# Transposes moved to another PSUM bank, and the last product of a feed-forward block in two column halves

## The chip, the cores and the metric

The kernel runs on one core of a Trainium2 chip. A core has five engines that run their own instruction queues and meet through semaphores: TensorE (PE in the profile, its weight loads PEld), VectorE (DVE), ScalarE (ACT), GpSimd (POOL) and SyncE (SP, which here only issues DMAs). Matmul results go to PSUM, eight banks of 512 fp32 values per partition; VectorE and ScalarE copy them out. The metric is device time of the whole program in microseconds (us), lower is better, and a kernel's time is the median of several runs.

## The reference

Clustered attention, followed by a feed-forward block with a leaky activation. Queries and keys are assigned to the nearest of 16 centroids per head; a query attends only to keys of its own cluster.

```python
q_assign = np.argmax(np.einsum('bhsd,hcd->bhsc', q_n, c_n), axis=-1)
k_assign = np.argmax(np.einsum('bhsd,hcd->bhsc', k_n, c_n), axis=-1)
mask = q_assign[:, :, :, None] == k_assign[:, :, None, :]
scores = scale * np.matmul(q, k.transpose(0, 1, 3, 2))
scores = np.where(mask, scores, -1000000000.0)
attn = np.exp(scores - np.max(scores, axis=-1, keepdims=True))
attn = attn / (np.sum(attn, axis=-1, keepdims=True) + 1e-09)
attn_out = np.matmul(attn, v)
x = attn_out.transpose(0, 2, 1, 3).reshape(B * S, H * D)
h = x @ w_in
g = np.maximum(h, 0.0) + alpha * np.minimum(h, 0.0)
out = g @ w_out
```

There are 4 batches (B), 8 heads (H), 768 tokens (S), head dimension 64; the model width DM is 512 and the hidden width 2048.

## The kernel before

Heads go in pairs, four pairs per batch, 16 in all (n = 0 to 15). For the first three batches each pair is computed whole: scores by matmul, exp on ScalarE, a mask on VectorE, the product with v on TensorE, and a division by row sums. For the last batch (n = 12 to 15) the tokens of each head are first sorted by cluster, so that each block of 128 keys needs only its neighbouring blocks of queries. The sorted result must then go back to token order. This way back is:

- `normalise_near` (L929) multiplies the two halves of the pair's result by the inverse sums and puts the rest into the plan with `later(slots, piece)`: `to_rows` for the first half 6 slots on, for the second half 9 slots on.
- `to_rows` (L951) transposes three 128x128 blocks of a half on TensorE (L955) into one PSUM bank; one slot later ScalarE copies them to `rows` (L958).
- `put_back` (L961) scatters rows to DRAM by an indirect DMA on GpSimd's queue (L963), 12 per pair; `fetch_back` (L968) loads them again by four DMAs on SP's queue (L975), and VectorE turns them into `xT` (L985).

Around this runs the feed-forward block of the batch before. `ffn_pieces` (L1000) makes a list of pieces per half batch: `hidden(f)` (L1013) makes 128 hidden units by four matmuls (L1017), which ScalarE copies out of PSUM as `gT` (L1023) and VectorE gives its slope (L1009); `final(i, f0, ...)` (L1028) multiplies the gT of several f with w_out (L1035). After the first eight f its result is copied to `y` (L1041), after the second eight it is added (L1043) and stored by SP (L1046). The main loop takes a slot at a time: it runs what is due (`tick`), then a piece of the attention, then as many feed-forward pieces as the plan wants (`feed`). Every engine runs its instructions in the order in which this program wrote them.

PSUM's eight banks are shared out by hand: `ps_s` two tiles of two banks for scores (`sps`), `ps_v` one bank (`vps`) for the product with v, `ps_m` one bank (`mps`) and `ps_f` two banks (`fps`). `fps` holds the feed-forward pieces, two of six score blocks in the last batch, and the transposes of `to_rows`. `mps` is what `misc()` (L84) gives: the sums over rows (`total`, L848), the cluster numbers (`prep_clusters`, L442), the second side of the product with v in the sorted batch (L926), and the small products of the check at the end (L1283, L1319). A new tile in a bank waits until the last reader of the tile before it has finished.

At the very end a flag `bad` is read by every engine (L1326), and all jump over a general version of the kernel that these inputs do not need (L1451). The last feed-forward half batch (b = 3, half = 1) runs alone there, after all attention: 8 hidden pieces, 6 final pieces, twice.

Of the kernel before, what the change touches and what calls it, by code (L numbers as in the profile page):

```python
# [10 lines left out]
FP32 = mybir.dt.float32  # L11
# [5 lines left out]
ALU = mybir.AluOpType  # L17
AX = mybir.AxisListType
PS = bass.MemoryType.PSUM
P = 128  # L20
# [3 lines left out]
def kernel(  # L24
# [11 lines left out]
    nc = tc.nc  # L36

    B, H, S, D = q.shape
    NC = centroids.shape[1]
    DM, DF = moe_w_in.shape  # L40
    NJ = S // P
    NCH = DM // P
    NF = DF // P
    HJ = NJ // 2
# [12 lines left out]
    w_out_sb = wpool.tile([P, NF, DM], FP32, name="w_out_sb")  # L57
# [9 lines left out]
    accp = fast.enter_context(tc.tile_pool(name="accp", bufs=2))  # L67
# [7 lines left out]
    ps_f = fast.enter_context(tc.tile_pool(name="ps_f", bufs=2, space=PS))  # L75
# [8 lines left out]
    def misc():  # L84
        if early:
            early.append(early.pop(0))
            if early[0] is not None:
                return early[0]
        return ps_m.tile([P, 512], FP32, name="mps")
# [5 lines left out]
    def later(slots, piece):  # L95
        due.setdefault(now[0] + slots, []).append(piece)
# [12 lines left out]
    Q = 32  # L109
# [52 lines left out]
    for g in range(P // Q):  # L162
        r = slice(g * Q, (g + 1) * Q)
        nc.gpsimd.tensor_copy(
            out=fold[r, :].rearrange("p (a i) -> p a i", i=Q),
            in_=ident[r, None, r].broadcast_to((Q, P // Q, Q)))
# [11 lines left out]
    for h in range(2):  # L178
        nc.vector.tensor_reduce(
            out=pick[:, h:h + 1],  # L180
            in_=fold.rearrange("p (a h c) -> p a h c", h=2, c=NC)[:, 0, h, :],
# [95 lines left out]
    FQ = CW // P  # L277
# [34 lines left out]
    def convert_up_to(n):  # L312
        while converted[0] < n:
            if not under_way:
                convert_next()
            else:
                advance(under_way[0])
# [54 lines left out]
    NX = GT * NG  # L372
# [556 lines left out]
    def normalise_near(n):  # L929
        outT = inp.tile([P, 2, NJ, D], FP32, name="qk").rearrange("p h j d -> p (h j d)")  # L930
        for side in range(2):
            nc.vector.tensor_tensor(out=outT[:, side * HS:(side + 1) * HS],
                                    in0=pos.pop((n, side))[:, 0:HS],
                                    in1=rds.pop((n, side)), op=ALU.mult)
        whole = tc.dram_tile([2 * S, D], FP32, name=f"back{n}")
        to = dram_disjoint_views(whole, 2 * NJ)
        found = orders.pop(n)
        place = sorts["order"].tile([P, 2, NJ], I32, name="place")
        nc.vector.tensor_scalar(out=place, in0=found[:, :, :, 0], scalar1=0, scalar2=S - 1,
                                op0=ALU.max, op1=ALU.min)  # L940
        rows = sorts["byrow"].tile([P, NJ, P], FP32, name="rows")

        starts = (6, 9)
        for i in range(2):
            later(starts[i], lambda i=i: to_rows(outT, rows, i))
            for x in range(NJ):
                later(starts[i] + 2 + x // 2,
                      lambda i=i, x=x: put_back(to, place, rows, i * NJ + x))
        later(starts[1] + 2 + HJ, lambda: fetch_back(n, whole))

    def to_rows(outT, rows, i):  # L951

        ps = ps_f.tile([P, 512], FP32, name="fps")
        for j in range(HJ):
            nc.tensor.transpose(out=ps[:, j * P:(j + 1) * P],  # L955
                                in_=outT[:, (i * HJ + j) * P:(i * HJ + j + 1) * P],
                                identity=ident)
        later(1, lambda: nc.scalar.copy(  # L958
            rows[:, i * HJ:(i + 1) * HJ].rearrange("p j d -> p (j d)"), ps[:, 0:HS]))
# [40 lines left out]
    def ffn_pieces(b, half):  # L1000
        rows = out[b * S:(b + 1) * S, :].rearrange(
            "(p j) n -> p j n" if b == 0 else "(j p) n -> p j n", p=P)
        gs, pss, ys, fresh = {}, {}, {}, deque()


        def slopes():
            while fresh:
                f = fresh.popleft()
                nc.vector.scalar_tensor_tensor(  # L1009
                    out=gs[f], in0=gs[f], scalar=alpha[:, f:f + 1], in1=gs[f],  # L1010
                    op0=ALU.mult, op1=ALU.max)

        def hidden(f):  # L1013
            convert_up_to((f // FQ + 1) * (NCH + FQ) - FQ)
            ps = ps_f.tile([P, 512], FP32, name="fps")
            for c in range(NCH):
                nc.tensor.matmul(out=ps[:, 0:HS],  # L1017
                                 lhsT=w_in_sb[:, c, f * P:(f + 1) * P],
                                 rhs=xTs[b, half][:, c, :],
                                 start=(c == 0), stop=(c == NCH - 1))  # L1020
            slopes()
            gs[f] = gpool.tile([P, HS], FP32, name="gT")
            nc.scalar.copy(gs[f], ps[:, 0:HS])  # L1023
            fresh.append(f)
            if f % FQ == FQ - 1:
                slopes()

        def final(i, f0, on, off):  # L1028
            convert_up_to((f0 // FQ + 1) * (NCH + FQ))
            if on:  # L1030
                pss[i] = ps_f.tile([P, 512], FP32, name="fps")
            unfinished[0] = not off
            ps = pss[i]
            for f in range(f0, f0 + FQ):
                nc.tensor.matmul(out=ps[:, 0:DM], lhsT=gs[f][:, i * P:(i + 1) * P],  # L1035
                                 rhs=w_out_sb[:, f, :], start=on and f == f0,
                                 stop=off and f == f0 + FQ - 1)
            if off:
                if i not in ys:
                    ys[i] = ypool.tile([P, DM], FP32, name="y")  # L1040
                    nc.scalar.copy(ys[i], ps[:, 0:DM])  # L1041
                else:
                    nc.vector.tensor_tensor(out=ys[i], in0=ys[i], in1=ps[:, 0:DM],  # L1043
                                            op=ALU.add)
                if f0 + FQ == NF:
                    nc.sync.dma_start(out=rows[:, half * HJ + i, :], in_=ys[i])  # L1046

        hs = [lambda f=f: hidden(f) for f in range(NF)]


        FP = FQ if (b, half) == (0, 0) else NF // 2
        pieces = []
        for f0 in range(0, NF, FP):
            pieces += hs[f0:f0 + FP]
            pieces += [lambda i=i, f=f, f0=f0: final(i, f, f == f0, f + FQ == f0 + FP)
                       for i in range(HJ) for f in range(f0, f0 + FP, FQ)]
        return pieces


# [70 lines left out]
    def feed_block(u):  # L1130
        n, half, _ = steps[u - 1]
        for i in (range(2) if half is None else (half,)):
            ffn.extend(ffn_pieces(pairs[n][0], i))

    def kept(block):


        return {NS // UB - 2: 4, NS // UB - 1: 12}.get(block, 0)

    for u in range(-AHEAD, TOGETHER):  # L1140
        for piece in load_at.get(u, []):
            piece()
        n, half, s = steps[max(u, 0)]
# [48 lines left out]
    for u in range(TOGETHER, NS + 1):  # L1192
        for piece in load_at.get(u, []):
            piece()
        if u < NS:
            n, half, s = steps[u]
# [49 lines left out]
        for i in slots:  # L1246
# [5 lines left out]
            pieces = len(ffn) - kept(u // UB) + -whole * left // (UB // SB * FREE)  # L1252
# [28 lines left out]
    ps = misc()  # L1281
    for i, p0 in enumerate((0, 1, P // 2, P // 2 + 1)):
        nc.tensor.matmul(out=ps[0:m, i * NN:(i + 1) * NN], lhsT=ident[:, p0:p0 + m],  # L1283
                         rhs=sorts["begins"], start=True, stop=True)
# [4 lines left out]
                            in1=ident[0:m, m - 1:m], op=ALU.add)  # L1289
# [4 lines left out]
    for i in (1, 3):  # L1294
# [13 lines left out]
                            op=ALU.subtract)  # L1308
    nc.vector.tensor_tensor(out=ends[:, 1, :], in0=ends[:, 1, :], in1=spans[:, 2, :],
                            op=ALU.subtract)  # L1310
# [9 lines left out]
                     start=True, stop=True)  # L1320
# [161 lines left out]
```

## Time and profile before

| | us |
|---|---|
| median of 5 runs | 992.65 (991.38 to 992.96) |
| the profiled execution | 992.19 |
| its span in the profile | 990.4 |
| TensorE busy | 967.3 (98%) |
| VectorE busy | 635.2 (64%) |
| ScalarE busy | 258.6 (26%) |
| hidden products, L1017, 1024 records | 343.7 |
| final products, L1035, 768 records | 339.2 |
| transposes, L955, 24 records | 4.1 |
| copies of them, L958, 8 | 0.478 to 0.513 each |

An fp32 matmul is two records in the trace, a transpose one. Records of TensorE overlap: one begins when the columns of the one before it have passed, while its own recorded end is modelled and later. So the distance between starts tells the pace. In the lines of the timeline the first number is the start, the second the length of the group, "x" the records in it, and the bracket tells idle time before it and who ended that. In the lines of waits the numbers are total us, times, longest us.

The eight groups of transposes (two for each of n = 12 to 15) start at 712.3, 716.4, 735.9, 740.1, 762.1, 765.9, 784.9 and 791.8 us. From 819 us on there are feed-forward pieces alone.

### The profile page before, as it was taken

How to read it: one execution, taken by the hardware profiler on the slowest of the kernel's cores; microseconds unless marked ns; L12 is line 12 of the kernel's file. 1: busy time of each engine (PE TensorE's matmuls, PEld its weight loads, DVE VectorE, ACT ScalarE, POOL GpSimd, SP SyncE). 2: the span in 40 equal slices, each digit the busy share in tenths (PEclk: the TensorE clock that was granted, in tenths of full speed). 3: DMA queues.
4: the chain of work that ended last, by engine and by line, in shares of the span. 5: the costliest groups of instructions: out<-in, count | busy, mean ns of one | idle time of the engine just before them, and what ended most of it. 6: DMA issues, size and time to landing. Idle time of an engine off the chain costs nothing.

```text
span 990.4 us, 10869 instructions
## 1 busy us (share of the span) xinstructions
PE 967.3 (98%) x3947; PEld 481.3 (49%) x3947; DVE 635.2 (64%) x1143; ACT 258.6 (26%) x468; POOL 210.1 (21%) x249
## 2 busy tenths in 40 slices
PE   8989999999999999999999999999999999999997
PEld 5534444445454454545445444454554545455453
DVE  5897788598487776877858788677997432011020
ACT  5665443223121221312222122231232101110110
POOL 2323222010000634301000263630055430000000
PEclk9999999999999999999999999999999999999999
DMA  7434655041200362416020121720531110000000
GB/s 284 133 127 130 136 132 77 17 88 24 33 1 24 97 104 56 85 37 110 1 32 1 51 79 36 131 57 11 86 66 34 31 52 11 0 11 22 0 1 34
DMA packets 174285, 60.45 MB, mean 61 GB/s; under 512 B 161216, under 2 KB 164752, under 8 KB 174224
## 3 DMA queue, kind: packets, MB, share of 16 engines
q1 hardware_dynamic: 168768, 51.42, 24.2%
q0 software_dynamic: 4608, 7.87, 2.4%
q8 instruction: 33, 0.54, 0.2%
q10 hardware_dynamic: 848, 0.39, 0.2%
q14 instruction: 28, 0.23, 0.1%
HBM read 45.15 MB, written 14.16 MB: 60 GB/s over the span
## 4 chain that ended last, share of the span: by engine, by line
PE 91%; DVE 5%; ACT 1%; issue 1%; POOL 0%; ACTq 0%; DVEq 0%; POOLq 0%
PE fps L1017 33%; PE fps L1035 33%; PE vps L893 9%; PE sps L757 8%; PE fps L757 3%; PE mps L381 1%; PE vps L926 1%; PE sps L766 1%; PE mps L926 1%; PE fps L354 1%; DVE power L265 1%; ACT gT L1023 1%; PE vps L201 0%; DVE w_in_sb L268 0%; PE mps L848 0%
## 5 line engine op out<-in xcount | busy, mean ns | idle before, releaser
L1017 PE MATMUL fps<-xT,w_in_sb 128*128 128x384 f32 x1024 | 343.7, 491 | 4.1 <-ACT gT L1023 2.0
L1035 PE MATMUL fps<-w_out_sb,gT 128*128 128x512 f32 x768 | 339.2, 596 | 1.1 <-DVE gT L1009 1.1
L1017 PEld LDWEIGHTS fps<-xT,w_in_sb 128*128 128x128 f32 x1024 | 190.7, 190 | 144.4 <-issue 6.3
L1035 PEld LDWEIGHTS fps<-w_out_sb,gT 128*128 128x128 f32 x768 | 143.5, 190 | 172.2 <-issue 161.8
L1009 DVE SCALAR_TENSOR_TENSOR gT<-gT,alpha 128x384 f32<-128x384 f32 x128 | 80.6, 636 | 143.4 <-ACT gT L1023 143.0
L663 POOL DMA_INDIRECT scratch<-stage,off x96 | 99.1, 1033 | 326.2 <-DMA stage<-in_v_dram 268.3
L1023 ACT COPY gT<-fps 128x384 f32<-128x384 f32 x128 | 61.2, 478 | 339.3 <-PE fps L1017 339.3
L757 PE MATMUL sps<-qkT 64*128 64x384 f32 (+1 forms) x512 | 96.4, 495 | 2.4 <-ACT E L778 2.4
L798 DVE SCALAR_TENSOR_TENSOR more<-aq,key,more 128x384 f32<-128x384 bf16 (+1 forms) x136 | 74.3, 605 | 29.3 <-ACT more L778 19.0
L778 ACT ACTIVATE E<-sps 128x768 f32<-128x768 f32 (+1 forms) x81 | 61.2, 803 | 70.4 <-PE sps L766 38.4
L963 POOL DMA_INDIRECT back<-rows,place x48 | 48.5, 1010 | 100.8 <-ACT rows L958 87.3
L757 PEld LDWEIGHTS sps<-qkT 64*128 64x128 f32 x512 | 45.8, 187 | 47.7 <-issue 18.7
L893 PE MATMUL vps<-E,vt 128*64 128x384 f32 x356 | 67.0, 503 | 1.7 <-DVE xT L993 1.7
L798 DVE SCALAR_TENSOR_TENSOR E<-aq,key,E 128x384 f32<-128x384 bf16 (+1 forms) x104 | 56.5, 600 | 16.1 <-ACT E L778 11.4
L1043 DVE TENSOR_TENSOR y<-y,fps 128x512 f32<-128x512 f32 x30 | 20.5, 685 | 69.9 <-PE fps L1035 69.9
L808 DVE TENSOR_TENSOR acc<-acc,E 128x768 f32<-128x768 f32 x47 | 44.9, 955 | 16.6 <-ACT E L778 15.3
L1041 ACT COPY y<-fps 128x512 f32<-128x512 f32 x24 | 14.1, 586 | 139.2 <-PE fps L1035 139.2
L778 ACT ACTIVATE more<-sps 128x768 f32<-128x768 f32 (+1 forms) x47 | 35.4, 797 | 41.2 <-PE sps L757 40.6
L893 PEld LDWEIGHTS vps<-E,vt 128*64 128x64 f32 x356 | 23.3, 138 | 34.1 <-issue 31.4
L893 PE MATMUL vps<-more,vt 128*64 128x384 f32 x220 | 38.8, 491 | 0.0
L271 POOL TENSOR_TENSOR w_in_sb<-w_in_sb,power 128x512 f32<-128x512 f32 x16 | 22.8, 1427 | 72.9 <-DVE w_in_sb L268 72.9
L757 PE MATMUL fps<-qkT 64*128 64x384 f32 x160 | 34.6, 509 | 0.0
(177 smaller groups left out, 708.6 us busy)
## 6 DMA issues: line engine op xcount, KB each, us to landing
raw<-in_moe_w_in_dram SPq DMA_DIRECT2D x16, 512.0 KB, 4.4
raw<-in_moe_w_out_dram SPq DMA_DIRECT2D x16, 512.0 KB, 3.5
out_dram<-y SPq DMA_DIRECT2D x24, 256.0 KB, 2.1
vt<-in_v_dram SPq DMA_DIRECT2D x12, 384.0 KB, 4.9
qk<-in_q_dram SPq DMA_DIRECT2D x48, 96.0 KB, 3.5
qk<-in_k_dram SPq DMA_DIRECT2D x48, 96.0 KB, 3.6
qk<-scratch SPq DMA_DIRECT2D x32, 96.0 KB, 3.3
qk<-in_q_dram SPq DMA_DIRECT2D x4, 384.0 KB, 8.7
```

Of the source, the lines that this page charges most:

```text
L271: nc.gpsimd.tensor_tensor(out=dst, in0=dst, in1=power[0].bitcast(FP32), op=ALU.mult)
L663: nc.gpsimd.indirect_dma_start(out=scratch[n][1][h * NX + xx], out_offset=bass.IndirectOffsetOnAxis(ap=ranks[n][:, xx, h:h + 1], axis=0), ...
L757: nc.tensor.matmul(out=bank(ps, h, m), lhsT=qkT[r:r + D, S + c * P:S + (c + 1) * P], rhs=qkT[r:r + D, tokens], start=True, stop=not early_ ...
L778: nc.scalar.activation(out=E[:, :, 0:m], in_=ps[:, :, 0:m], func=AF.Exp, scale=SCALE)
L798: nc.vector.scalar_tensor_tensor(out=e, in0=of, scalar=keys[n][:, NJ + c, h:h + 1], in1=e, op0=ALU.is_equal, op1=ALU.mult)
L808: nc.vector.tensor_tensor(out=acc, in0=acc if first is None else first[3], in1=E, op=ALU.add)
L893: nc.tensor.matmul(out=po[r:r + D, 0:HS], lhsT=vts[n][:, h, c, :], rhs=e[:, h, :], start=(c == 0), stop=(c == NJ - 1))
L963: nc.gpsimd.indirect_dma_start(out=to[i], out_offset=bass.IndirectOffsetOnAxis(ap=place[:, h, j:j + 1], axis=0), in_=rows[:, j, h * D:(h + ...
L1009: nc.vector.scalar_tensor_tensor(out=gs[f], in0=gs[f], scalar=alpha[:, f:f + 1], in1=gs[f], op0=ALU.mult, op1=ALU.max)
L1017: nc.tensor.matmul(out=ps[:, 0:HS], lhsT=w_in_sb[:, c, f * P:(f + 1) * P], rhs=xTs[b, half][:, c, :], start=(c == 0), stop=(c == NCH - 1))
L1023: nc.scalar.copy(gs[f], ps[:, 0:HS])
L1035: nc.tensor.matmul(out=ps[:, 0:DM], lhsT=gs[f][:, i * P:(i + 1) * P], rhs=w_out_sb[:, f, :], start=on and f == f0, stop=off and f == f0 + ...
```

## The change

`to_rows` takes its bank from `misc()`, that is `mps`, instead of `ps_f`. For the last half batch, the two last pieces (the second eight f of row block i = 2, in two groups of four f, over all 512 columns) become two pieces over all eight f and 256 columns each. Each half has its own bank, is added to its half of `y` into a tile of the pool `accp`, and is stored on its own: the first half from SP's queue, the second from ScalarE's.

```diff
     def to_rows(outT, rows, i):
 
-        ps = ps_f.tile([P, 512], FP32, name="fps")
+        ps = misc()
         for j in range(HJ):
             nc.tensor.transpose(out=ps[:, j * P:(j + 1) * P],
...
+        def final_columns(i, f0, c0):
+
+            ps = ps_f.tile([P, 512], FP32, name="fps")
+            c = slice(c0, c0 + DM // 2)
+            for f in range(f0, NF):
+                nc.tensor.matmul(out=ps[:, 0:DM // 2], lhsT=gs[f][:, i * P:(i + 1) * P],
+                                 rhs=w_out_sb[:, f, c], start=f == f0, stop=f == NF - 1)
+            y = accp.tile([P, 2 * NX, Q], FP32, name="acc").rearrange(
+                "p x i -> p (x i)")[:, 0:DM // 2]
+            nc.vector.tensor_tensor(out=y, in0=ys[i][:, c], in1=ps[:, 0:DM // 2], op=ALU.add)
+            (nc.scalar if c0 else nc.sync).dma_start(out=rows[:, half * HJ + i, c], in_=y)
+
...
+        if (b, half) == (B - 1, 1):
+
+            pieces[-(FP // FQ):] = [lambda c0=c0: final_columns(HJ - 1, NF - FP, c0)
+                                    for c0 in (0, DM // 2)]
         return pieces
```

## The prediction

> **What bounds the kernel now.** I read the page first: busy shares, then the chain.
>
> ```profile
> PE 967.3 (98%) x3947; PEld 481.3 (49%) x3947; DVE 635.2 (64%) x1143; ACT 258.6 (26%) x468; POOL 210.1 (21%) x249
> PE 91%; DVE 5%; ACT 1%; issue 1%; POOL 0%; ACTq 0%; DVEq 0%; POOLq 0%
> ```
>
> TensorE (PE) is busy for 98% of 990.4 us and 91% of the chain. So time can be won in two ways only: PE stalls that vanish, and what comes after PE's last matmul. Next, PE's own waits between 700 and 800 us, the stretch in which the transposes run:
>
> ```profile
> PE fps L1017 <- ACT gT L1023: 2.0, 6, 0.6
> PE fps L955 <- ACT gT L1023: 1.1, 2, 0.6
> PE fps L1017 <- ACT y L1041: 0.7, 1, 0.7
> ```
>
> All three end when ScalarE (ACT) has emptied an fps bank. Idle counts only what a matmul's recorded tail does not cover, so I measured stalls by starts. The pace comes from the chain in order of time: "L1017 x64" in 20.64 us is 0.322 us a record, "L1035 x48" in 20.60 us is 0.429, and L955's three records stand 0.109 apart; a line through these gives 0.215 for 256 columns. A matmul is two records. The first round, PE and then ACT:
>
> ```profile
> 712.26 0.49 PE L955 MATMUL fps<-ident,qk 128*128 128x128 f32 x3
> 712.99 2.85 PE L1017 MATMUL fps<-xT,w_in_sb 128*128 128x384 f32 x8 [0.24 <-ACT gT L1023]
> 716.41 0.55 PE L955 MATMUL fps<-ident,qk 128*128 128x128 f32 x3 [0.57 <-ACT gT L1023]
> 716.79 2.85 PE L1017 MATMUL fps<-xT,w_in_sb 128*128 128x384 f32 x8
> 719.48 0.25 PE L442 MATMUL mps<-cluster,spread 128*128 128x24 bf16 x4
> ...
> 712.46 0.48 ACT L1023 COPY gT<-fps 128x384 f32<-128x384 f32 x1 [1.80 <-PE fps L1017]
> 715.88 0.48 ACT L1023 COPY gT<-fps 128x384 f32<-128x384 f32 x1 [2.94 <-PE fps L1017]
> 716.25 0.49 ACT L958 COPY rows<-fps 128x384 f32<-128x384 f32 x1
> ```
>
> The transposes T1 (712.26) take one of the two fps banks. Unstalled, the next hidden piece would start at 712.26 + 3 x 0.109 = 712.59; it starts at 712.99, after the gT copy. Also, the first record after such a wait is followed 0.427 instead of 0.322 later, as its second weight load had not run ahead: 0.105 more. A stall thus costs its wait plus about 0.1. Note the order on ACT: the copy of T1 (L958) stands behind the gT copy of the next piece.
>
> Last, the end of the kernel:
>
> ```profile
> 984.38 0.69 DVE L1043 TENSOR_TENSOR y<-y,fps 128x512 f32<-128x512 f32 x1 [6.18 <-PE fps L1035]
> 985.09 0.33 SPq L1046 DMA_DIRECT2D out_dram<-y  x1
> DMA to landing us min/median/max: 3.3/3.3/3.3
> L1451 ACTq COMPARE_BRANCH  x1: 54/54/54, 964.3 to 964.3; - x1
> L1451 ACTq EVENT_SEMAPHORE  x1: 17/17/17, 966.9 to 966.9; - x1
> L1451 DVEq COMPARE_BRANCH  x1: 72/72/72, 985.0 to 985.0; - x1
> L1451 DVEq EVENT_SEMAPHORE  x1: 21/21/21, 988.4 to 988.4; - x1
> ```
>
> PE ends at T = 984.34. The last store lands at 988.4, though 256 KB stores have a median of 2.1 us; then SP checks its semaphores one by one and the span ends at 990.4, T + 6.06. Each engine then jumps over the general version, and its next instruction comes late: 2.6 us on ACT, 3.4 on VectorE (DVE).
>
> **Part A, the transposes in mps.** Nothing is added: the same 24 transposes and 8 copies at the same places in each queue. What changes is who waits. Hidden pieces no longer lose a bank to T1 or T2. But mps is one bank, so T2 waits for the ACT copy of T1, and whatever uses mps next waits for the copy of T2. I step through the four rounds; times are those of before, each round taken from its own T1.
>
> Round 1 (712.26). The piece starts at 712.59; its eighth record at 714.85, ending 0.49 later; gT copy from 715.37; copy of T1 0.37 behind it, 715.74 to 716.23; T2 at 716.28 (before 716.41); next piece 716.66, with no 0.1 behind it. L442 (sorts' clusters) then needs mps, which the copy of T2 frees at 720.30: L442 at 720.35 instead of 719.48. Four records and the exposed load put the following piece's second record at 720.93, before 720.63. Loss 0.30.
>
> Round 2 (735.92). T2 at 739.94 by the same steps (before 740.07), no 0.1 behind it: L1035's second record at 740.75, before 740.99. Gain 0.24. The sum (L848) that takes mps next comes 7 us later.
>
> Round 3 (762.06). The wait for the y copy before 770.48 goes: 1.268 from the record before, of which 0.429 is due, so 0.84, plus 0.10. But 2.6 us later L848 waits for DVE's row sums (L835), which end at 772.75 after DVE has been busy without a gap since 761.6. PE would be there at 772.22 and was there at 773.16. So the stall moves to DVE, and by the second record of the next piece 0.30 is left. If that wait did not bind, 0.94.
>
> Round 4 (784.93). T1 and T2 stand two pieces apart, so the copy of T1 (788.41 to 788.90) is done long before T2 (790.41). Four stalls go: 0.404, 0.732 and 0.405 with 0.104 behind each: 1.85.
>
> Sum of A: -0.30 + 0.24 + 0.30 + 1.85 = 2.1 us; bounds 1.5 (round 1 loses 0.6, round 3 gains nothing) and 2.8 (round 3 whole). What this is hidden by: nothing, PE is the chain. What comes earlier on other queues: POOL's twelve scatters (L963) of the last round and SP's four loads (L975) behind them start about 0.7 us earlier, while the flag's matmul (L1319, at 818.99) comes 2.1 earlier. Its input (L1315) ended at 816.06, so some 1.5 us of slack stay, and the last xT (811.7) has more.
>
> **Part B, the last product by halves.** PE: 16 records at 0.429 = 6.86 become 32 at 0.215 = 6.89. Weight loads of 128 columns start 0.11 apart at the L848 sums (747.43, 747.53), so they hide under 0.215. No row shows 128x128 weights with 256 columns: bounds 0.215 and 0.295 a record (a load of 0.19 plus the exposed 0.105), 0 to 2.5 us; I take 0.03, since the 0.109 spacing is the nearer row.
>
> After T: the add of 256 columns is 0.42 (L818's 128x256 row), not 0.69. The first half's add and SP's store lie 3.4 us earlier, under PE, and are free. ACT's store starts at T + 0.48. Behind it on ACT's queue stand only the flag's load (0.48) and the jump, which before ran at 964. So ACT now jumps at the end: issue 0.33 (SP's price) to 0.60 (L474, ACT's), load 0.48 to 0.54, branch 0.1, gap 2.6 (ACT's row) to 3.4 (DVE's): ready at T + 4.0 to T + 5.2, and from a late engine's arrival to the end are about 1.1 us (SP's last checks from 989.3, and the closing handshake). That is T + 5.1 to T + 6.3. The store lands at T + 0.48 + 1.9 to 3.8 (L474's median and maximum) = T + 2.4 to T + 4.3, and SP's checks take the 1.95 they took: T + 4.3 to T + 6.2. The later of the two against T + 6.06: between 0.95 won and 0.25 lost. I take 0.7 won, near ACT's own row.
>
> On the jump the Trainium skill (Runtime: NRT & Kernel Launch, Instruction fetch mechanics) says that a taken branch to a page not loaded must first fetch it by DMA; this speaks against giving ACT the last store, and the rows above agree with it (2.6 and 3.4 us), though the page has no price. It also says (DMA: Bandwidth & Descriptors, Rules for kernel authors) that two transfers of disjoint partition halves are not worth the bother (here it is halves of the columns); by its fit for one DMA, 2.0 us plus bytes over 436 GB/s, the smaller store lands an estimated 0.3 us sooner, and by that alone B would win 0.3.
>
> **Sum.** 2.1 + 0.7 - 0.03 = 2.8 us. The profiled execution took 992.19, 1.8 around its span of 990.4; its span should become 987.6. The median of the runs is 992.65, 0.5 above that execution, so 989.9 us. A measurement of this kernel tells 0.2% (2.0 us) from no change.
>
> **Rivals.**
> 1. The tail gives nothing: ACT's jump takes DVE's 3.4 us. For it: two fetches then fall together with the store. Against: ACT's own row. Time 992.65 - 2.1 = 990.6, on the 0.2% border.
> 2. The change does not free the bank: "free" slots are not free, since ACT's order puts every copy of T1 behind a gT copy. For it: round 1. If round 4 too loses half (0.9) and round 3 gains nothing, A is 0.9 and the tail 0.3: 991.4, within 0.2%. Against: in round 4 T1 and T2 have two pieces between them.
> 3. Every stall goes, DVE's and L442's too: by starts rounds 1 to 4 hold 2.1 + 1.4 + 0.9 + 1.9 = 6.3 us; with 0.9 of tail 985.5. Against: the in-order waits worked out above.
> 4. Slower: a 256-column record is paced by its weight load and not by its columns. At the full 0.429 the last product doubles, 6.87 us more: 992.65 - 2.8 + 6.9 = 996.7. It decides from 0.215 + 2.8 / 32 = 0.30 a record upward. Against: loads 0.109 apart.
>
> **How the numbers follow.** Forecast 0.64; rival 1 0.13; rival 2 0.12; rival 3 0.05; rival 4 0.06. Rival 1 is half faster, half within 0.2%. Faster 0.64 + 0.05 + 0.06 = 0.75, same 0.12 + 0.07 = 0.19, slower 0.06. The forecast's terms run from 1.5 - 0.25 = 1.3 to 2.8 + 0.95 = 3.8 us, so 988.9 to 991.3; I widen the lower end by 0.2 for the median's own spread: 988.7 to 991.3. This leaves out rivals 2 to 4 (0.23, rival 2 partly inside).
>
> **What would show it.** A: no PE wait of L1017 on gT after a transpose; L442 some 0.9 us after the piece before it; L848 of round 3 waiting for DVE L835; round 4's pieces following at 0.322 without gaps. B: 32 records 0.215 apart; ACT's jump the last to end, about T + 4. The prediction is wrong if PE shows new waits on rows L958 in rounds 2 or 4, if L1319 waits, or if the end comes later than T + 6.1.

## The result, and the profile after

The changed kernel takes 989.9 us in the median (989.05 to 992.99, 26 runs) against 992.5 (991.09 to 994.68, 47 runs) for the kernel before: ratio 0.9977, 95% interval 0.9972 to 0.9983. That is 2.6 us by the medians and 2.3 by the ratio, and the predicted number. TensorE still bounds it, as two lines of the page of the changed kernel show:

```profile
PE 968.2 (98%) x3963; PEld 484.9 (49%) x3963; DVE 635.1 (64%) x1144; ACT 258.6 (26%) x468; POOL 210.6 (21%) x249
PE 91%; DVE 6%; ACT 1%; issue 1%; POOL 0%; ACTq 0%; DVEq 0%; POOLq 0%
```

There are 16 PE records more (32 of 256 columns in place of 16 of 512), and one more add on VectorE.

The profiled execution took 992.67 us with a span of 990.9, about the same as the one before (992.19 and 990.4), though the medians differ by 2.6. This is a matter of the execution and not of the change: up to the first transposes both kernels run the same instructions, and yet the first transposes start at 714.64 and not at 712.26. Three windows of both kernels are shown. The columns are the window, its length, busy time of the five engines with the number of instructions, the granted clock of TensorE, DMA share and rate; the changed kernel is first, then the one before.

```profile
46.00:50.00 4.00, 4.00 (x26) 1.66 (x21) 3.18 (x5) 0.61 (x2) 1.60 (x2) 0.60 0.71 241
62.00:72.00 10.00, 8.09 (x60) 3.40 (x64) 8.82 (x18) 6.68 (x11) 5.27 (x4) 0.83 0.56 179
84.00:92.00 8.00, 5.18 (x12) 2.70 (x11) 6.69 (x17) 1.08 (x3) 2.73 (x2) 0.79 0.28 93
```

```profile
46.00:50.00 4.00, 3.75 (x46) 2.09 (x46) 3.84 (x5) 1.92 (x4) 2.26 (x2) 1.00 0.69 215
62.00:72.00 10.00, 7.05 (x64) 2.84 (x64) 9.65 (x19) 7.21 (x11) 4.36 (x4) 1.00 0.61 204
84.00:92.00 8.00, 6.61 (x21) 3.66 (x20) 6.54 (x18) 2.17 (x5) 2.85 (x2) 1.00 0.39 111
```

TensorE had a lower clock in all three stretches of this execution: 0.60, 0.83 and 0.79 against 1.00. Instruction by instruction, the changed kernel's execution is 0.66 us ahead at 46 us, 0.95 behind at 55, 2.39 behind at 100, and stays at 2.38 up to the transposes. So the time is lost in and near these stretches; that the clock is the cause is argued, not shown. So the two traces are compared from the first transposes on. From there to the end of the last matmul (T) the kernel before takes 984.338 - 712.260 = 272.08 us, the changed one 984.732 - 714.638 = 270.09.

The waits of PE between 700 and 800 us, changed kernel:

```profile
PE mps L955 <- ACT rows L958: 1.9, 2, 1.0
PE mps L442 <- ACT rows L958: 0.9, 1, 0.9
PE mps L848 <- ACT gT L1023: 0.5, 1, 0.5
```

Not one wait on an fps bank is left; before, three lines of them held 3.8 us. In their place PE waits for the copy of the transposes (L958), which now frees mps. The timeline of the changed kernel shows it for round 1, PE first, then ACT:

```profile
714.64 0.49 PE L955 MATMUL mps<-ident,qk 128*128 128x128 f32 x3
714.97 2.75 PE L1017 MATMUL fps<-xT,w_in_sb 128*128 128x384 f32 x8
718.66 0.55 PE L955 MATMUL mps<-ident,qk 128*128 128x128 f32 x3 [0.95 <-ACT rows L958]
719.05 2.75 PE L1017 MATMUL fps<-xT,w_in_sb 128*128 128x384 f32 x8
722.74 0.25 PE L442 MATMUL mps<-cluster,spread 128*128 128x24 bf16 x4 [0.95 <-ACT rows L958]
...
717.75 0.48 ACT L1023 COPY gT<-fps 128x384 f32<-128x384 f32 x1 [2.43 <-PE fps L1017]
718.12 0.48 ACT L958 COPY rows<-mps 128x384 f32<-128x384 f32 x1
721.83 0.48 ACT L1023 COPY gT<-fps 128x384 f32<-128x384 f32 x1 [3.22 <-PE fps L1017]
722.21 0.48 ACT L958 COPY rows<-mps 128x384 f32<-128x384 f32 x1
```

The piece behind T1 starts 0.33 after it, with no gap. But T2 waits until 718.66, although the transposes T1 were done by 715.13: their copy stands on ACT behind the gT copy of a piece that ends only at 717.7. L442 waits in the same way for the copy of T2. So ACT's order, not its speed, sets these waits, 1.9 us (rounds 1 and 2) and 0.9 us; experiment 3 tests this. One line of PE from each of the other rounds, T2 of round 2, the row sums of round 3 and T2 of round 4:

```profile
742.56 0.55 PE L955 MATMUL mps<-ident,qk 128*128 128x128 f32 x3 [0.95 <-ACT rows L958]
775.29 0.39 PE L848 MATMUL mps<-parts,fold 128*128 128x48 f32 x2 [0.52 <-ACT gT L1023]
792.62 0.49 PE L955 MATMUL mps<-ident,qk 128*128 128x128 f32 x3
```

Round 4 has no wait left. The profile puts the wait of L848 down to ACT's gT copy; experiment 8 shows that it is VectorE's.

The end, from the timeline of the changed kernel (line numbers behind the new function are 16 higher: L1467 was L1451):

```profile
984.77 0.42 DVE L1057 TENSOR_TENSOR acc<-y,fps 128x256 f32<-128x256 f32 x1 [3.03 <-PE fps L1053]
985.22 0.38 ACTq L1058 DMA_DIRECT2D out_dram<-acc  x1
```

and from the rows of L1058 and L1467:

```profile
DMA to landing us min/median/max: 3.5/3.6/3.8
```

```profile
L1467 PEldq COMPARE_BRANCH  x1: 4042/4042/4042, 981.3 to 981.3; - x1
L1467 DVEq EVENT_SEMAPHORE  x1: 21/21/21, 988.7 to 988.7; - x1
L1467 ACTq EVENT_SEMAPHORE  x1: 17/17/17, 989.3 to 989.3; - x1
```

The add takes 0.42 in place of 0.69, ACT issues the last store at T + 0.49, and half as many bytes are stored. Still the store lands at T + 4.26 (before: T + 4.10) and the span ends at T + 6.16 (before: T + 6.07). In this execution the halves won nothing; why, experiments 2, 5 and 6 show.

### The profile page after: what moved, and what is told of

Its sections match the earlier page's. It is cut to its first block, busy times and chain, and to the rows that moved or that the text cites. A ratio compares the mean times of both kernels' runs of the same rounds, so it can differ in the third digit from the quotient of the medians.

```text
span 990.9 us, 10896 instructions
## 1 busy us (share of the span) xinstructions
PE 968.2 (98%) x3963; PEld 484.9 (49%) x3963; DVE 635.1 (64%) x1144; ACT 258.6 (26%) x468; POOL 210.6 (21%) x249
## 4 chain that ended last, share of the span: by engine, by line
PE 91%; DVE 6%; ACT 1%; issue 1%; POOL 0%; ACTq 0%; DVEq 0%; POOLq 0%
PE fps L1017 33%; PE fps L1035 32%; PE vps L893 8%; PE sps L757 8%; PE fps L757 3%; PE mps L381 1%; PE vps L926 1%; PE sps L766 1%; PE fps L1053 1%; PE mps L926 1%; DVE power L265 1%; PE fps L354 0%; PE vps L201 0%; DVE w_in_sb L268 0%; DVE power L253 0%
## 5 line engine op out<-in xcount | busy, mean ns | idle before, releaser
L1035 PE MATMUL fps<-w_out_sb,gT 128*128 128x512 f32 x752 | 332.2, 596 | 1.1 <-DVE gT L1009 1.1
L1035 PEld LDWEIGHTS fps<-w_out_sb,gT 128*128 128x128 f32 x752 | 140.5, 190 | 168.3 <-issue 158.0
L757 PE MATMUL sps<-qkT 64*128 64x384 f32 (+1 forms) x512 | 98.7, 505 | 2.4 <-ACT E L778 2.4
```

The costliest lines, as they stand in the source:

```text
L757: nc.tensor.matmul(out=bank(ps, h, m), lhsT=qkT[r:r + D, S + c * P:S + (c + 1) * P], rhs=qkT[r:r + D, tokens], start=True, stop=not early_ ...
```

## The experiments

Twelve runs were made, ten of other kernels and two (9 and 10) of the same two again. "PE part" is the time from the first transposes to T, "tail" from T to the end of the span, both of the profiled execution.

| kernel | median us | ratio [95%] | PE part | tail |
|---|---|---|---|---|
| before | 992.5 | | 272.08 | 6.07 |
| changed | 989.9 | 0.9977 [0.9972, 0.9983] | 270.09 | 6.16 |
| 1 bank alone | 990.39 | 0.9971 [0.9961, 0.9982] | 270.06 | 5.96 |
| 2 halves alone | 992.82 | 1.0001 [0.9992, 1.0009] | 272.12 | 5.11 |
| 3 changed, copy at once | 987.28 | 0.9945 [0.9931, 0.9960] | 267.16 | 5.26 |
| 4 before, copy at once | 989.82 | 0.9967 [0.9954, 0.9980] | 269.58 | 5.50 |
| 5 both stores on SP | 990.37 | 0.9982 [0.9971, 0.9993] | 270.10 | 5.12 |
| 6 cut at 128 and 384 | 991.38 | 0.9984 [0.9973, 0.9995] | 270.14 | 5.31 |
| 7 bank, copy at once, no halves | 987.98 | 0.9957 [0.9943, 0.9971] | 267.11 | 5.73 |
| 8 as 3, turn two slots later | 985.80 | 0.9936 [0.9921, 0.9952] | 265.89 | 5.66 |
| 9 before again (see below) | 997.68, one run | | 273.86 | 6.06 |
| 10 changed again | 992.77, one run | | 271.66 | 5.34 |
| 11 as 8, no halves | 991.43 | 0.9961 [0.9948, 0.9974] | 268.84 | 5.98 |
| 12 as 8, both stores on SP | 991.51 | 0.9961 [0.9948, 0.9975] | 274.31 | 5.40 |

The last four ran on another chip, beside runs of the kernel before that took 995.54 us in the median, 3.0 more than elsewhere. So their times are compared only with each other, and their ratios are to that 995.54.

### 1. The bank alone

```diff
-        ps = ps_f.tile([P, 512], FP32, name="fps")
+        ps = misc()
```

Expected: 

> Only the transposes go through mps; the last product and its store are as before. Theory 1 (the gain is the bank, worth 2.0 us by the starts of the four rounds, and the halves are worth about nothing): 2.0 us under before, ratio 0.9980, every round's steps as in the changed kernel, the end as before at 6.1 us behind PE's last matmul. Rival (the halves bring a share of the measured 2.3 us): 1.3 us or less under before, ratio 0.9987 or more.

Measured: ratio 0.9971, the PE part 2.02 us shorter than before, as in the changed kernel (270.06 and 270.09). PE's waits between 700 and 800 us are line for line those of the changed kernel. What the change wins on PE is this one line.

### 2. The halves alone

```diff
+        if (b, half) == (B - 1, 1):
+            pieces[-(FP // FQ):] = [lambda c0=c0: final_columns(HJ - 1, NF - FP, c0)
+                                    for c0 in (0, DM // 2)]
```

with the transposes left in fps. Expected:

> Only the last product goes by halves with two stores, the second from ScalarE; the transposes stay in fps. Theory 1 (the end is set by a store whose share on one DMA engine waits behind an instruction fetch, so halves win nothing): ratio 0.9998 to 1.0003, the end 6.0 to 6.3 us behind PE's last matmul. Rival (halves win 0.7 us, and the changed kernel's profile was an odd one): ratio 0.9993, the end 5.1 to 5.5 us behind PE's last matmul.

Measured: ratio 1.0001. PE's part is 0.04 longer, and all of the old waits for fps are there. The tail of the profile is 5.11, though, 0.96 shorter than before. In the rows of L1467 of this kernel ACT is the last engine to come back from its jump, 4.15 after T = 986.86 and 0.96 before the end:

```profile
L1467 DVEq EVENT_SEMAPHORE  x1: 21/21/21, 990.6 to 990.6; - x1
L1467 ACTq EVENT_SEMAPHORE  x1: 17/17/17, 991.0 to 991.0; - x1
```

So the halves can win almost 1 us in one execution and nothing in another, and over many runs this experiment can't tell their worth from zero.

### 3 and 4. The copy written right behind the transposes

Round 1 says that ACT's order is what holds T2 and L442. This edit changes that order alone, in the changed kernel (3) and, in the bank of before, in the kernel before (4):

```diff
-        later(1, lambda: nc.scalar.copy(
-            rows[:, i * HJ:(i + 1) * HJ].rearrange("p j d -> p (j d)"), ps[:, 0:HS]))
+        nc.scalar.copy(rows[:, i * HJ:(i + 1) * HJ].rearrange("p j d -> p (j d)"), ps[:, 0:HS])
```

Expected of 3:

> The changed kernel, but ScalarE's copy of the transposes is written right behind them and not a slot later, so it stands before the next piece's gT copy in ScalarE's queue. Theory 1 (the waits that are left in rounds 1 and 2, 1.115, 1.113 and 1.114 us by starts, come from that order on ScalarE): they go, 2.5 to 3.3 us under the changed kernel, ratio to before 0.9943 to 0.9955; the wait of L848 in round 3 on DVE's row sums stays. Rival (one bank is too little whatever the order, or VectorE sets the pace of these rounds): within 1 us of the changed kernel, ratio 0.9968 to 0.998.

Expected of 4:

> The kernel before, transposes in fps, with the one edit that ScalarE's copy is written right behind the transposes. Theory 1 (order on ScalarE costs as much as the shared bank): T1's bank comes free some 3 us earlier, which by the starts saves 1.1 in round 1, 0.4 in round 2, 0.3 in round 3 and 0.8 in round 4: 2.6 us under before, ratio 0.9974, as good as the move to the other bank; the waits of 0.4 us of a hidden piece on the gT copy before it stay. Rival (only the bank counts): no change, ratio 0.9995 to 1.0005.

Measured of 3: 987.28, the PE part 2.93 us shorter than with the change. Its timeline (line numbers behind L958 are one lower):

```profile
712.80 0.49 PE L955 MATMUL mps<-ident,qk 128*128 128x128 f32 x3
...
715.71 0.49 PE L955 MATMUL mps<-ident,qk 128*128 128x128 f32 x3
...
718.62 0.25 PE L442 MATMUL mps<-cluster,spread 128*128 128x24 bf16 x4
...
744.96 0.39 PE L848 MATMUL mps<-parts,fold 128*128 128x48 f32 x2 [0.27 <-DVE parts L835]
...
770.52 0.39 PE L848 MATMUL mps<-parts,fold 128*128 128x48 f32 x2 [0.53 <-ACT gT L1022]
```

T2 and L442 follow without a wait, 2.91 and 5.82 us after T1 (in the changed kernel 4.02 and 8.10). By starts the three waits that go were 1.115, 1.114 and 1.113 us, 3.34 together; 0.11 more goes behind two of them (the second transpose after such a wait came 0.06 late), and 0.44 + 0.08 comes back as a new wait of L848 in round 2, since PE now arrives before VectorE has the row sums. Together that is the measured 2.93.

Measured of 4: ratio 0.9967, the PE part 2.50 us shorter. The copy's order alone, with the transposes still in fps, is worth as much as the change of bank (2.02 by PE's part; by time the intervals overlap). The waits of PE between 700 and 800 us of this kernel:

```profile
PE fps L1016 <- ACT gT L1022: 1.2, 5, 0.2
PE mps L848 <- DVE parts L835: 0.4, 1, 0.4
PE fps L1034 <- ACT gT L1022: 0.2, 1, 0.2
```

Six short waits of pieces for a bank are left here, about 0.2 of idle time each (by starts 0.405, and 0.104 behind each), and these are what the change of bank removes. Together the two edits win 4.92 on PE's part.

### 5 and 6. What holds the end

5 is the changed kernel with both stores on SP's queue, 6 with the last product cut at 128 and 384 columns:

```diff
-            (nc.scalar if c0 else nc.sync).dma_start(out=rows[:, half * HJ + i, c], in_=y)
+            nc.sync.dma_start(out=rows[:, half * HJ + i, c], in_=y)
```

```diff
-                                    for c0 in (0, DM // 2)]
+                                    for c0, w in ((0, DM // 4), (DM // 4, 3 * DM // 4))]
```

Expected of 5:

> The change with both stores of the last product on SP's queue, so that ACT has no late jump (it should jump near T - 20 as before the change). T is the end of PE's last matmul; the changed kernel's tail in its own profile was 6.16 us, with the last store landing at T + 4.26 and ACT back from its jump at T + 4.52; with the halves alone it was 5.11 (landing T + 3.06, ACT back at T + 4.15). Theory A, the store's slowest share sets the end (it stands behind an instruction fetch on its DMA engine): the tail stays landing + 1.9, that is 5.0 to 6.2, whatever queue issues the store, and SP's own jump, which moves back behind the store as before the change (its fetch near T + 2), makes it no shorter. Theory B, ACT's jump sets the end: without it the tail falls to 4.9 to 5.1, set by DVE's jump (back at T + 3.8 to 4.1, about 1.0 before the end). Either way the time differs from the changed kernel's by less than a measurement can tell (989 to 991).

Expected of 6:

> The change with the last product cut at 128 and 384 columns instead of 256 and 256. PE's queue reads ahead by some 16 records: its jump was issued at T - 7.28 before the change (17 records of 0.429) and at T - 3.43 with halves (16 of 0.2155). Its second instruction fetch (16 KB, 3.2 to 3.8 us after the first) therefore fell at T - 3.1 before, and at T + 0.7 to T + 1.4 with halves, onto the last store. With a last piece of 384 columns the jump should be issued near T - 5.2 and the second fetch at T - 0.9 or before, done before the store's packets start at about T + 1.5. Theory A (PE's fetch holds the store): landing at T + 2.6 to 3.0 and a tail of 5.0 to 5.3 set by ACT's jump; PE is back at T + 0.04. Rival (some other thing holds the store's one late share): landing at T + 3.1 or later all the same. Records of 128 columns 0.11 apart and of 384 0.322, so PE takes 6.9 as before. Time within what a measurement can tell of the changed kernel's.

The DMA packets of the traces tell more than the landing time. A store is 144 packets here, which fall into 16 shares of nine (eight of data and one of 4 bytes). In every profile 15 shares were written by T + 1.8 to T + 2.4, and one came later; that one's packets begin when an instruction fetch has ended. This table is worked out from the DMA packets, all times after T:

```text
kernel              fetch: whose, start, took, end    late share begins   landing   tail
before              DVE's jump   2.24  0.31  2.56     2.55                4.10      6.07
before, again       DVE's jump   2.23  0.31  2.54     2.54                4.09      6.06
1 bank alone        DVE's jump   1.72  0.75  2.47     2.47                3.98      5.96
4                   DVE's jump   1.70  0.65  2.36     2.35                3.53      5.50
7                   DVE's jump   1.77  0.68  2.45     2.44                3.76      5.73
11                  DVE's jump   1.71  0.79  2.50     2.50                4.00      5.98
changed             PE's, 16 KB  1.35  1.74  3.09     3.09                4.26      6.16
changed, again      PE's, 16 KB  1.06  1.22  2.28     2.26                3.44      5.34
2 halves alone      PE's, 16 KB  0.88  1.04  1.93     1.91                3.06      5.11
3                   PE's, 16 KB  0.72  1.47  2.19     2.17                3.36      5.26
8                   PE's, 16 KB  1.07  1.50  2.57     2.56                3.75      5.66
5 both on SP        PE's, 16 KB  1.02  0.96  1.98     1.97                3.21      5.12
12 both on SP       PE's, 16 KB  0.81  1.44  2.24     2.23                3.49      5.40
6 128 and 384       DVE's jump   1.71  0.57  2.28     2.28                3.40      5.31
```

The beginning agrees with the fetch's end within 0.02 us in all 14. It does so as well for the first half's store in the seven kernels with equal halves: in the changed kernel PE's first fetch lies from T - 2.42 to T - 0.83, and that store's late share begins at T - 0.84. Stores without a fetch beside them are the control. Of the output stores of the 14 profiles, 153 have packets that can be told apart. 44 of them have a share that ends more than 0.3 us behind the others, and each of these has a fetch in the time of its packets. Of the 109 without such a share, 103 have no fetch there, and in the other six the fetch ends as the packets begin or begins as they end.

Two things stay open. The records name neither the DMA engine of a packet nor the owner of a fetch, so that the share and the fetch lie on one DMA engine is inferred, and a fetch is put down to the engine whose jump comes before it. And where the fetch is PE's, it began (T + 0.72 to 1.35) before the other shares did (T + 1.31 to 1.46); but the fetch behind VectorE's jump began at T + 1.70 to 2.24, later than the other shares (T + 1.51 to 1.68), and what held the late share until then isn't shown.

The end of the span follows the landing by 1.90 in seven of the eight profiles with a divided last product and by 1.97 in the six without. Only in experiment 2 is it 2.05; there ACT, back at T + 4.15, is the later one.

Why it is PE's fetch where the product is halved is told by the jump's rows. PE's queue reads ahead of the array and meets the jump some records early: 16 records have still to start at that time in the kernel before, 15 in the changed one, 13 with 384 columns (experiment 6). The kernel before:

```profile
L1451 PEldq COMPARE_BRANCH  x1: 3426/3426/3426, 977.1 to 977.1; - x1
```

That is T - 7.28; in the changed kernel (981.3, shown above) it is T - 3.43, as 15 records of 0.2155 take about half as long as 16 of 0.429. PE's second fetch, 16 KB, 3.1 to 3.8 us after the first, so moved from T - 3.1 to T + 1.35: from before the store to the place where the store's packets are.

Measured of 5: tail 5.12, landing + 1.91. ACT had jumped at 963.1 and nobody waited for it. Without ACT's jump the tail is no shorter than the best one with it (5.11). In the changed kernel's profile ACT was back 1.64 before the end, against 0.96 in experiment 2, so that jump isn't what holds it at 6.16; the landing is. The time of 5 can't be told from the changed kernel's.

Measured of 6: PE's jump came at T - 4.67 (expected T - 5.2) and its fetch ended at T + 0.75, before the store's packets began. But the landing was T + 3.40 and not 2.6 to 3.0: the fetch behind VectorE's jump (T + 1.71 to 2.28) took the place of PE's. So in number the rival's forecast came true (T + 3.1 or later), but the share again begins with a fetch's end, which is the first theory's mechanism: VectorE makes the last add and jumps right behind it, and its fetch was the next. Rows of L1467 of this kernel:

```profile
L1467 PEldq COMPARE_BRANCH  x1: 3578/3578/3578, 980.6 to 980.6; - x1
L1467 DVEq COMPARE_BRANCH  x1: 72/72/72, 985.9 to 985.9; - x1
```

### 7. What the halves add to the better version

This is experiment 3 without final_columns (its diff is the reverse of 2's). Expected:

> Transposes in mps with the copy written right behind them, and the last product whole as before the change. Against the same with halves (987.28, ratio 0.9945): if the halves win their 0.3 to 0.9 us in the tail on average, this one takes 987.6 to 988.2 (ratio 0.9948 to 0.9955) and its tail is 5.5 to 6.1; if the halves give nothing, 987.3. By the stalls PE ends its last matmul at the same place as the one with halves, 0.04 earlier.

Measured: 987.98 against 987.28, intervals overlapping; the PE parts are 267.11 and 267.16, the tails 5.73 and 5.26. The sign is that of a small win, but the times can't tell it from nothing; between experiment 1 and the changed kernel the sign is the other way (0.9971 and 0.9977).

### 8. The turn behind the row sums

```diff
-        later(4 if n == NP - 1 else 9, turn_back)
+        later(4 if n == NP - 1 else 11, turn_back)
```

on top of experiment 3. Expected:

> The change with the copy written right behind the transposes, and the turn of the rows fetched back (DVE, 1.03 us) two slots later, so that it stands behind the row sums and not in front of them. Theory (what is left of rounds 2 and 3 is VectorE's load, not the bank): the two waits of the sums over rows for DVE, 0.436 + 0.075 and 0.689 + 0.075 us by starts, go, and PE ends 1.2 to 1.3 us sooner: 986.0, ratio about 0.993. Rival (DVE is late for another reason, or the moved turn delays what DVE does next): the waits stay within 0.2 us of what they were, or new ones of the same size come behind, at the inverse sums or at the slopes, and the time stays 987.3.

Measured: 985.8 us, ratio 0.9936, the fastest. The PE part is 1.28 us shorter than in 3, as expected, and no wait of PE is left between 700 and 800 us. From its timeline:

```profile
744.57 0.32 PE L848 MATMUL mps<-parts,fold 128*128 128x48 f32 x2
...
769.36 0.32 PE L848 MATMUL mps<-parts,fold 128*128 128x48 f32 x2
...
743.10 0.95 DVE L835 TENSOR_REDUCE parts<-acc 128x24 f32<-128x768 f32 x1
...
744.87 1.00 DVE L984 STREAM_TRANSPOSE xT<-qk 128x384 f32<-128x384 f32 x2
```

The turn (L984) now lies behind the row sums (L835), and L848 waits in neither round. This also settles who held L848 in round 3: the line of waits named ACT's gT copy, but in this kernel only VectorE's order has changed, and the wait is gone.

### 9 to 12. The same kernels again, and the halves on the best version

9 and 10 are the kernels before and after as they are. 11 is experiment 8 without the halves, 12 experiment 8 with both stores on SP. Expected, in this order:

> The kernel before as it is, one more profiled execution: from the first transposes to the last matmul 272.08 us (984.34 - 712.26) within 0.15, so 2.0 more than the changed kernel; tail 5.5 to 6.1, its store's late share beginning where the fetch for VectorE's jump ends.

> The changed kernel as it is, one more profiled execution. In ten profiles so far the first transposes start at 712.3 to 713.3 us in seven and at 714.6 to 715.1 in three, though all ten kernels have the same instructions up to there. If that is a matter of the execution and not of the kernel, this one starts them at either place, and from there to the last matmul takes the same 270.1 us (984.73 - 714.64) within 0.15. The store's late share begins when an instruction fetch on its DMA engine ends, to within 0.05 us, and the tail lies between 5.1 and 6.2.

> Copy written right behind the transposes, turn two slots later, last product whole: the best kernel so far (985.8, ratio 0.9936) without the halves. If the halves are worth what the tails of the profiles show (mean of four without 5.82, of five with equal halves 5.46, so 0.36 us), 986.2; if nothing, 985.8; if 0.9, 986.7. PE's part from the first transposes to its last matmul as in the one with halves, 265.9 us within 0.15; tail 5.5 to 6.1.

> The best kernel so far with both stores of the last product on SP's queue: PE's part 265.9 us; tail 5.0 to 5.7, set by the store's share behind PE's second fetch or by DVE's jump (back 3.7 to 4.2 after the last matmul), since ACT jumps early. Time 985.3 to 985.9; against the one with ACT's store (985.8) less than can be told.

What held: the late share of the store (table above) and the tails. The first transposes do start at different times in executions of the same code (715.92 and 713.90 here; 712.3 to 716.1 over all 14 profiles), but at neither of the two places that were named. In all four of these profiles 1.0 to 1.1 us are lost between 629 and 643 us, against the kernel before instruction by instruction; without that they would lie at 712.2 to 715.1, where the ten others lie. What failed: PE's parts were not within 0.15 us of those seen before, but 1.78, 1.57, 2.95 and 8.42 longer. The time is lost between 726 and 740 us. The worst case, on ACT and PE in experiment 12:

```profile
733.63 0.48 ACT L1022 COPY gT<-fps 128x384 f32<-128x384 f32 x1 [7.29 <-remote]
...
734.17 1.65 PE L757 MATMUL fps<-qkT 64*128 64x384 f32 x2 [4.62 <-issue]
```

The copy's input was done at 727.63. The trace doesn't name what ACT waited for, and this stays open, as does the loss at 629 us. Experiment 9 shows that the kernel before loses time in the same places; all four ran on the other chip, and no profile from elsewhere shows it. Against the kernel before beside them, 11 and 12 are 0.39% faster, less than the 0.64% of experiment 8. With such losses 11 and 12 tell nothing apart (991.43 and 991.51), so the worth of the halves on the best version stays unsettled by time. The profiles give an estimate: the tails of the six with a whole last product have a mean of 5.88 us (5.50 to 6.07), those of the seven with equal halves 5.44 (5.11 to 6.16), a win of 0.45 with a standard error of about 0.17. The five of these seven that store from ACT, as the change does, have 5.51, a win of 0.38 with 0.21.

## Why the prediction was right, step by step

**What bounds the kernel** was right: only PE stalls and the tail moved the time, and from 800 us to the end PE waits for nothing, so POOL's scatters and the flag's matmul never came onto the path.

**The bank, round by round.** Each round's change is read as the shift of its start from that of the next, changed kernel against before:

| | predicted | measured | how |
|---|---|---|---|
| round 1 | -0.30 | -0.23 | shift of T1 grows from 2.378 to 2.612 |
| round 2 | +0.24 | +0.22 | falls to 2.388 |
| round 3 | +0.30 | +0.19 | falls to 2.202 |
| round 4 | +1.85 | +1.85 | falls to 0.354 at the next L1035 |
| sum | 2.1 | 2.02 | |

Round 1 is a loss, as stepped through: T2 and L442 wait for L958. In round 3 the stall moved to L848 behind VectorE, as said; there 0.11 less was won than predicted. In round 4 three stalls went, as many as its sum adds up (its words say four). One sign of error that the prediction named, a wait on L958 in round 2, did appear (0.95 at 742.56); the step for round 2 had itself reckoned with it, so it was the sign that was badly chosen. That PE would lose 0.03 by 32 records of 256 columns was right too (0.04 in experiment 2): they start 0.2155 apart, and rival 4 with its 0.30 and more falls.

**The tail** is the term that was mis-sized. The two candidates were right and so were their bounds: ACT back at T + 4.15 to T + 4.52 where T + 4.0 to T + 5.2 was said, the landing at T + 3.06 to T + 4.26 where T + 2.4 to T + 4.3 was said. But I took ACT's jump as the later one and 0.7 us as won. That step failed: in seven of the eight profiles with a divided last product the landing came last, and ACT's jump only in experiment 2. Measured against before's profile it is -0.09 in the changed kernel's own profile, which also passes the T + 6.1 that was named as a sign of error; 0.73 in its second, 0.96 in experiment 2, and 0.45 as the mean of all profiles (0.38 with ACT's store alone). What the step didn't see is that PE's jump moves too, 3.85 us nearer to the end, since its queue runs ahead by records and these became shorter; one share of the store then begins only when PE's fetch has ended. On such jumps the Trainium skill (Runtime: NRT & Kernel Launch, Instruction fetch mechanics) says that the sequencer fetches code by a DMA queue of its own in blocks of 16 KB; PE's fetches here are of 16,384 bytes and agree, those behind the other engines' jumps are of 8,192, and the table above shows what that means for a store at the same time. The 0.3 us that the prediction estimated from the page's fit counts bytes alone. That is near what the 15 other shares show: from issue to their last packet the half store took 1.42 where the whole one took 1.66 (the profiles of the changed kernel and of before), 0.24 less. The late share is not in that estimate, and it moves the landing by up to 1.2 (T + 3.06 to 4.26).

**The sum** of 2.8 became 2.02 + 0.4 - 0.04 = 2.4 us; the medians differ by 2.6. That the predicted 989.9 was met to the digit is luck: 0.4 was missing, but the median of the kernel before, 992.5, was in the end 0.15 lower than in the five runs that the sum started from, and the rest is within what a median of this kernel tells. The range and the part on the bank are not luck.

**The rivals.** Rival 1 (nothing from the tail) is what experiment 1 is, and its 990.6 is met by 990.39; as a story of the change it lies about 0.4 away from the mean of the profiles and can't be excluded by time. Rival 2 named ACT's order, copy of T1 behind a gT copy; that mechanism is there in rounds 1 and 2 and costs 3.34 us, but round 4 won its whole 1.85, so the price was wrong. Rival 3 (every stall goes, 6.3 us on PE) isn't what the change does, but experiment 8 does it: 272.08 - 265.89 = 6.19 us, at 985.8 against the 985.5 worked out.

## What to carry to other kernels

Where a buffer is waited for, look at what stands in front of its reader in the queue that frees it: moving the copy by one place was worth as much as another bank, and with both the next wait was again one of order, on VectorE. A stall that is removed ahead of an in-order consumer comes back at the next engine that is late; follow it there before counting it (of 3.34 us, 0.5 came back). And at the end of a program, shorter instructions shorten the time by which a queue runs ahead of its engine (here from 7.28 to 3.43 us), so that the jump's code fetch can fall onto the last store.

## What the runs showed of the hardware that was not expected

Where an instruction fetch fell into the time of a store, one of the store's 16 shares came late, as if one DMA engine served both. For the last store it came 0.6 to 1.9 us after the others in all 14 profiles, its first packet within 0.02 us of a fetch's end, and its landing set the end or came close to it. The 103 output stores with no fetch beside them had no such share.

The same instructions up to the first transposes took 712.3 to 716.1 us in 14 executions. In the five that were late (714.6 to 716.1: the changed kernel and experiments 2, 6, 9 and 12) the clock granted to TensorE was 0.60 to 0.66 between 46 and 50 us, in the nine others (712.3 to 713.9) it was 1.00. The Trainium skill (TensorE: Matmul & The Clock Gate, Part 1) says that the gate watches a window that runs free of the kernel and so differs from run to run; that fits, but no run here shows the window itself, nor that the clock alone made the difference. So one profile of each kernel may differ by more than an edit of 2 us is worth, and the traces have to be compared from a point behind such a stretch.
